# Linear attention and a feed-forward layer on one core: sums of g moved behind the fourth division, k^T v moved ahead of one product, a third way of computing block 2, and four sums of weights given to GpSimd

## The chip, the core and the metric

The kernel runs on one core of a Trainium2 chip. The core has a matrix engine (TensorE, "PE" in the profile, its weight loads "PEld"), a vector engine (VectorE, "DVE"), a scalar engine (ScalarE, "ACT"), GpSimd ("POOL") and a queue engine (SyncE, "SP"), each of which works through its own instructions in their written order. They wait for each other by semaphores. [...] The metric is the device time of one execution in microseconds (us), taken as the median of several; lower is better.

## The reference

With B = 8 batches, H = 8 heads, S = 576 positions and D = 64, the attention is linear, with cosine and sine weights by position; behind it stand two matrix products with a gelu between them:

```
phi(x) = concat(relu(x) * cos_w, relu(x) * sin_w)          # 64 -> 128 features
kv = phi(k)^T v ;  z = sum over positions of phi(k)
x  = (phi(q) kv) / (phi(q) z + 1e-6)                       # (8, 576, 512) -> 4608 tokens of 512
h  = x @ w_in                                              # 512 -> 2048
g  = h * sigmoid(1.702 h)
out = g @ w_out                                            # 2048 -> 512, (4608, 512) float32
```

## The kernel before, in words

A block is a batch. Of its 576 tokens 512 are worked on in the block; the last 64 of each batch are collected in `xt` and are the tail, done after all blocks. The order of all instructions is written out by hand (`manual_schedule`): what stands earlier in the program comes earlier in its engine's queue.

The blocks are staggered. While block b is in its matrix products, the attention of block nb = b + 1 is prepared: `trig` (L169) makes the weighted relu of k on VectorE, `vcopy` (L193) converts v, `trig_q` (L183) makes that of q on ScalarE, and `qturn_dma` (L219) turns it with a transposing DMA from SP's queue. `kv_next` opens a PSUM tile of the pool `pat` (name `at`), makes k^T v in 72 small matmuls (L237) and has VectorE copy it to `kvs` (L245). Five times per block, `x_next(nb, c)` then does for 128 tokens: `num_mm` (eight matmuls, L310, into a tile of `pat`), `num_div` (VectorE: L321 adds eps to the denominators, L323 inverts, L325 multiplies and writes `xn`) and `xturn_dma` (L354), a transposing DMA that writes the x of the next block. The pool `pat` has two buffers, so `num_mm` number c waits until VectorE has done with the division of number c - 2.

The first product of a block, x @ w_in, is done in 16 column groups fc of 128 columns. In the plain way (`mm1_part` at L365, `mm1_at` at L721) a group is four matmuls of 128 x 512. Blocks 3 to 6 (the range `PAIR`) use *units* instead for groups 0 to 3 and 8 to 11 (`mm1_pair`, class `Unit`): a form of fast matrix multiplication in which two units U and V make seven products (`step(1)` to `step(7)`, four matmuls of 128 x 256 each, L658) where the plain way needs eight. It needs sums of blocks of w_in (`win_sum`, L621 to L627, made once and kept in `ws_pair`, which lies in the buffer `gt`) and of blocks of x (`x_pair`, `x_sum`, L635 to L641, made for each block at the end of the block before). Between the products, ScalarE copies partial results (`snap`, L672) and VectorE adds (`add`, L667); the gelu of a unit reads such a sum (L663). Groups 4 to 7 and 12 to 15 remain plain. Block 2 does all 16 groups in the plain way, and during it VectorE makes the four sums of w_in.

The second product, g @ w_out, is done with seven products too (`wino_mm`, L520), in the order of `PRODUCTS`: p1, p2, p6, p5, p7, p3, p4. Each has two halves c, so the program counts s = 0 to 13. p6, p5, p7 and p3 take as their weights the sums s2, s1, s3 and s4 of blocks of g, which VectorE makes in `g_sums` (L473, L475, L477, L479), each in two halves h of 128 x 1024. `wino_after` has ScalarE keep a partial result (`keep`, L535) or VectorE join two into an output (`join`, L545); the output leaves by a DMA from GpSimd's queue (L526).

In a block of PAIR the last steps are, as written: `V.step(5)`, the plain group 14, `V.step(3)`, `kv_next`, the plain group 15, each with its gelu, then s1 and s2 for h = 0 and h = 1, `x_next(nb, 0)`, and the fourteen `wino_mm` with x_next 1 to 4 behind s = 1, 3, 4 and 6. The two halves of s3 stand behind s = 1, those of s4 behind s = 5.

Of the kernel before, what the change touches and what calls it, by code (L numbers as in the profile page):

```python
# [20 lines left out]
def kernel(  # L21
# [9 lines left out]
    nc = tc.nc  # L31
    B, H, S, D = q.shape
# [24 lines left out]
    def src_of(src, b, i0=0, i1=NI):  # L57
        return src[b, 2 * i0:2 * i1].rearrange("(i hh) (p j) d -> (hh p) i (j d)", hh=2, j=NS)

    qf = one.tile([128, 2560], F32, name="qf")  # L60
    kf, vf = [one.tile([128, NI, S], F32, name=n) for n in ("kf", "vf")]
# [62 lines left out]
    def load(t, src, b, eng=nc.gpsimd):  # L124
        eng.dma_start(out=t, in_=src_of(src, b))
# [7 lines left out]
    def load_q(b, eng=nc.gpsimd):  # L133
        load_chunks(qf, q, b, eng)
# [5 lines left out]
    def wcol(kc, fc):  # L140

        g, c = divmod(fc, 4)
        w = w_in_t[g][:, kc, :] if g < 2 else w_in_t[2][:, kc, ts(g - 2, 512)]
        return w.rearrange("p (f c) -> p f c", c=4)[:, :, c]
# [216 lines left out]
    def mm1_part(b, fc, t0, t1):  # L361
        if t0 == 0:
            hp[fc] = pmm.tile([128, MT], F32, name="mm")
        for kc in range(KC):
            nc.tensor.matmul(hp[fc][:, t0:t1], wcol(kc, fc), x[b][:, kc, t0:t1],  # L365
                             start=(kc == 0), stop=(kc == KC - 1))
# [99 lines left out]
    def g_sums(names, h, of=MAIN):  # L466

        tt = nc.vector.tensor_tensor
        a_blk, to = of
        o = {n: to[n][:, ts(h, 4)] for n in to}  # L470
        for n in names:
            if n == "s1":
                tt(o[n], a_blk(1, h), a_blk(1, h + 2), op=ADD)  # L473
            elif n == "s2":
                tt(o[n], o["s1"], a_blk(0, h), op=SUB)  # L475
            elif n == "s3":
                tt(o[n], a_blk(0, h), a_blk(1, h), op=SUB)  # L477
            else:
                tt(o[n], a_blk(0, h + 2), o["s2"], op=SUB)  # L479
# [119 lines left out]
    ws = {}  # L599
# [12 lines left out]
        slot_no[0] += 1  # L612
        return slots[slot_no[0] % 8].rearrange("p (f t) -> p f t", f=2)

    def win_sum(n, i, ws=ws):
        tt = nc.vector.tensor_tensor
        o = {m: ws[m][:, :, ts(i, 512)] for m in ws}
        a = {(0, k): w_in_t[i][:, ts(k, 2), :] for k in range(2)}
        a.update({(1, k): w_in_t[2][:, ts(k, 2), ts(i, 512)] for k in range(2)})
        if n == "s1":  # L620
            tt(o[n], a[1, 0], a[1, 1], op=ADD)  # L621
        elif n == "s2":
            tt(o[n], o["s1"], a[0, 0], op=SUB)
        elif n == "s3":
            tt(o[n], a[0, 0], a[1, 0], op=SUB)
        else:
            tt(o[n], a[0, 1], o["s2"], op=SUB)  # L627
# [15 lines left out]
    class Unit:  # L643
# [31 lines left out]
        def step(self, p):  # L675
# [17 lines left out]
            else:  # L693
# [2 lines left out]

    PAIR = range(3, B - 1)
    gt_flat = gt.rearrange("p f e -> p (f e)")  # L700
    ws_pair = {n: gt_flat[:, ts(i, 1024)].rearrange("p (k f) -> p k f", k=2)
               for i, n in enumerate(("s1", "s2", "s3", "s4"))}
# [15 lines left out]
    def mm1_at(b, fc):  # L718
        hp[fc] = pat.tile([128, 2, 512], F32, name="at")[:, 0]
        for kc in range(KC):  # L720
            nc.tensor.matmul(hp[fc], wcol(kc, fc), x[b][:, kc], start=(kc == 0), stop=(kc == KC - 1))  # L721
        gelu(fc, True)

    def mm1_pair(b, nb):
        for qd in (0, 2, 1, 3):
            gT[qd] = gpool.tile([128, 4, MT], BF16, name="g")
        banks4 = [pmm.tile([128, 512], F32, name="mm") for _ in range(4)]
        U, V = [Unit(b, u, banks4[u], banks4[2], banks4[3], ws_pair, xp[b], pair_slot) for u in range(2)]
        ks = iter(range(NS))

        def k_next(n):
            for _ in range(n):
                trig(kr, kf, next(ks))

        U.step(1)
        V.step(1)
        k_next(3)
        mm1_at(b, 4)
        mm1_at(b, 5)
        U.step(2)  # L740
        k_next(4)
        U.step(6)
        V.step(6)
        U.gelu(0, 0, U.c11)
        mm1_at(b, 6)
        mm1_at(b, 7)
        V.step(2)
        k_next(2)
        if nb + 1 < B:
            load_q(nb + 1, nc.sync)  # L750
            load(kf, k, nb + 1, nc.sync)
        U.step(7)
        U.step(5)
        V.gelu(0, 0, V.c11)
        V.step(7)
        mm1_at(b, 12)
        U.gelu(1, 1, U.c22)
        U.step(4)
        U.gelu(1, 0, U.A)
        vcopy(0, 2)  # L760
        U.step(3)
        vcopy(2, 4)
        V.step(4)
        V.gelu(1, 0, V.A)
        U.gelu(0, 1, U.c12)
        mm1_at(b, 13)
        V.step(5)
        mm1_part(b, 14, 0, MT)
        V.gelu(1, 1, V.c22)
        V.step(3)  # L770
        gelu(14)
        kv_next()
        mm1_part(b, 15, 0, MT)
        V.gelu(0, 1, V.c12)
        gelu(15)
        g_sums(("s1", "s2"), 0)
# [16 lines left out]
    def kv_next():  # L793
        kv_mm_next()
        kv_evac(0, 4)
# [169 lines left out]
    def x_next(b, c):  # L965
        num_mm(c)
        num_div(c)
        xturn_dma(b, c)


    for b in range(1, B):
        nb = b + 1 if b + 1 < B else None
        if nb is None:
            break
        f0 = 5 if b == 1 else 0
        if b in PAIR:
            mm1_pair(b, nb)
        for fc in range(f0, FC) if b not in PAIR else ():
            if b == 1 and fc == f0:
                for c in range(5):  # L980
                    trig_q(c)
                    qturn_dma(c)
            if nb is not None and fc == f0 + 1:
                kv_operands(nb)

                if nb + 1 < B:
                    if b == 1:
                        load(kf, k, nb + 1, nc.sync)
                    load_q(nb + 1, nc.sync)
                    if b > 1:  # L990
                        load(kf, k, nb + 1, nc.sync)
                if b == 2:
                    for n in ws_pair:
                        win_sum(n, 0, ws_pair)
            if fc == 8 and b == 1:
                vcopy()
            if fc == 12:
                if b > 1:
                    g_sums(("s3",), 0)
                    g_sums(("s3",), 1)  # L1000
                g_sums(("s1", "s2", "s4") if b > 1 else ("s1", "s2"), 0)
            if fc == 14 and nb is not None and b > 1:
                kv_next()
            mm1(b, fc)
        if nb is not None:
            x_open(nb)
            if b == 2:
                x_next(nb, 0)
            if b == 1:
                kv_mm_next()  # L1010
            g_sums(("s1", "s2"), 1)
            if b > 2:
                x_next(nb, 0)
            if b == 1:
                kv_evac(0, 4)
                g_sums(("s3",), 0)
            at = ({2: [0], 3: [1], 4: [2], 6: [3], 8: [4]} if b == 1 else
                  {2 * p + 1: [p + 1] for p in range(4)} if b == 2 else
                  {s: [p + 1 if nb < B - 1 else (4, 1, 2, 3)[p]] for p, s in enumerate((1, 3, 4, 6))})
            wino_open()  # L1020
            for p in range(7):
                for c in range(2):
                    wino_mm(p, c)
                    s = 2 * p + c
                    if c == 1:
                        wino_after(b, p)
                    for c2 in at.get(s, ()):
                        x_next(nb, c2)
                        if c2 == 3 and nb + 1 < B:
                            load(vf, v, nb + 1, nc.sync)  # L1030

                    s0 = 4 if b > 2 else 8
                    if s0 <= s < s0 + 5 and nb + 1 < B:
                        trig_q(s - s0, act=True)
                    if 8 <= s < 13 and nb + 1 < B:
                        qturn_dma(s - 8)
                    if s == 1 and b == 2:
                        g_sums(("s4",), 1)
                    if s == 1 and b > 2:
                        g_sums(("s3",), 0)  # L1040
                        g_sums(("s3",), 1)
                    if s == 5 and b > 2:
                        g_sums(("s4",), 0)
                        g_sums(("s4",), 1)
                    if s == 2 and b == 1:
                        g_sums(("s3",), 1)
                    if s == 4 and b == 1:
                        g_sums(("s4",), 0)
                    if s == 6 and b == 1:
                        g_sums(("s4",), 1)  # L1050
            if nb in PAIR:
                x_pair(nb)
# [3 lines left out]
    b = B - 1  # L1056
# [103 lines left out]
```

## Time and profile before

| what | value |
|---|---|
| median of 3 runs | 277.41 us (277.34 to 277.67) |
| the profiled execution | 277.53 us, span of its instructions 275.6 us |
| PE busy | 267.9 us (97% of the span), clock granted in full in all slices |
| VectorE busy | 203.0 us (74%) |
| ScalarE busy | 172.8 us (63%) |
| GpSimd busy | 43.0 us (16%), most of it issuing DMAs |
| block 1, second product | from 67.07 to 80.56 us on PE |
| block 2 | from 80.56 to 109.12 us on PE |
| block 3 | from 109.12 to 137.61 us on PE |
| tail and block 7 | from 223.24 us on |

Times in the views of the trace count from the start of the span. A row of the timeline merges equal neighbouring instructions of one engine: start, length, engine, line, operation, names of what is written and read, sizes, and how many; in brackets the idle time before it and what ended it. The ends of matmuls are modelled and overlap the next start, so on PE the distances between starts are to be read. The chain is the sequence of work, followed back from the last instruction, that ended last.

### The profile page before, as it was taken

How to read it: one execution, taken by the hardware profiler on the slowest of the kernel's cores; microseconds unless marked ns; L12 is line 12 of the kernel's file. 1: busy time of each engine (PE TensorE's matmuls, PEld its weight loads, DVE VectorE, ACT ScalarE, POOL GpSimd, SP SyncE). 2: the span in 40 equal slices, each digit the busy share in tenths (PEclk: the TensorE clock that was granted, in tenths of full speed). 3: DMA queues.
4: the chain of work that ended last, by engine and by line, in shares of the span. 5: the costliest groups of instructions: out<-in, count | busy, mean ns of one | idle time of the engine just before them, and what ended most of it. 6: DMA issues, size and time to landing. Idle time of an engine off the chain costs nothing.

```text
span 275.6 us, 6999 instructions
## 1 busy us (share of the span) xinstructions
PE 267.9 (97%) x2844; PEld 204.5 (74%) x2844; DVE 203.0 (74%) x476; ACT 172.8 (63%) x311; POOL 43.0 (16%) x71
## 2 busy tenths in 40 slices
PE   8899999999999999999999999999999999999994
PEld 2585645856975699778877887788778876999983
DVE  4943775698899596879887988888888985744741
ACT  6967642584297519974788387848683147677621
POOL 5691000000122012100210022001200163000310
PEclk9999999999999999999999999999999999999999
DMA  7999999999999897997799689999991754000233
GB/s 232 253 211 298 278 295 162 255 305 197 301 207 289 225 262 192 255 242 206 187 299 233 195 114 278 170 284 194 236 196 23 107 149 139 0 0 2 82 111 114
DMA packets 73663, 53.60 MB, mean 194 GB/s; under 512 B 52736, under 2 KB 63488, under 8 KB 73632
## 3 DMA queue, kind: packets, MB, share of 16 engines
q1 hardware_dynamic: 67504, 36.97, 60.9%
q0 software_dynamic: 6128, 16.19, 22.6%
q8 instruction: 22, 0.36, 0.6%
q14 instruction: 9, 0.07, 0.1%
HBM read 36.70 MB, written 9.44 MB: 167 GB/s over the span
## 4 chain that ended last, share of the span: by engine, by line
PE 81%; DVE 12%; DMA 4%; issue 1%; ACT 0%; POOL 0%
PE mm L520 22%; PE mm L365 16%; PE mm L658 14%; PE at L721 8%; PE mm L421 5%; PE at L520 4%; PE mm L396 4%; PE at L237 4%; DVE xn L325 3%; DMA sums<-in_v_dram 2%; DVE sums L475 2%; PE at L310 2%; DVE sums L477 2%; DVE sums L473 2%; DMA kf<-in_k_dram 1%; DVE inv L323 1%
## 5 line engine op out<-in xcount | busy, mean ns | idle before, releaser
L365 PE MATMUL mm<-xT,w_in 128*128 128x512 bf16 (+1 forms) x304 | 51.4, 320 | 0.0
L526 POOL DMA_DIRECT2D out_dram<-ysb x24 | 18.1, 754 | 182.0 <-DVE den L321 124.6
L520 PEld LDWEIGHTS <-sums 128*128 128x128 bf16 x448 | 42.5, 98 | 4.6
L371 ACT ACTIVATE g<-mm 128x512 bf16<-128x512 f32 x56 | 32.2, 597 | 14.6 <-PE mm L365 14.6
L365 PEld LDWEIGHTS <-w_in 128*128 128x128 bf16 x304 | 27.6, 114 | 17.3
L520 PE MATMUL mm<-wsum,sums 128*128 128x256 bf16 x336 | 39.9, 272 | 0.0
L520 PEld LDWEIGHTS <-g 128*128 128x128 bf16 x336 | 32.0, 98 | 3.6
L169 DVE TENSOR_SCALAR kr<-kf,cosw 128x256 bf16<-128x256 f32 x69 | 24.5, 355 | 5.3 <-DMA kf<-in_k_dram 5.3
L325 DVE TENSOR_TENSOR xn<-at,inv 128x512 bf16<-128x512 f32 x39 | 27.0, 691 | 1.3
L520 PE MATMUL mm<-w_out_sb,g 128*128 128x256 bf16 x224 | 26.6, 273 | 0.0
L169 DVE TENSOR_SCALAR kr<-kf,sinw 128x256 bf16<-128x256 f32 x68 | 23.5, 345 | 0.0
L721 PE MATMUL at<-xT,w_in 128*128 128x512 bf16 x96 | 23.3, 379 | 0.0
L183 ACT ACTIVATE qn<-qf,cosw 128x512 bf16<-128x512 f32 (+1 forms) x27 | 19.2, 712 | 2.2 <-DMA qf<-in_q_dram 2.2
L183 ACT ACTIVATE qn<-qf,sinw 128x512 bf16<-128x512 f32 (+1 forms) x27 | 19.2, 710 | 0.0
L535 ACT ACTIVATE kept_p<-mm 128x512 f32<-128x512 f32 (+1 forms) x15 | 8.5, 566 | 16.7 <-PE mm L520 14.9
L658 PE MATMUL mm<-xT,w_in 128*128 128x256 bf16 x128 | 18.6, 273 | 0.0
L658 PEld LDWEIGHTS <-w_in 128*128 128x128 bf16 x144 | 15.9, 113 | 2.7
L310 PEld LDWEIGHTS <-qT 128*128 128x128 bf16 x312 | 13.8, 97 | 5.1 <-issue 3.7
L658 PE MATMUL mm<-xT,gt 128*128 128x256 bf16 x128 | 17.2, 272 | 0.0
L310 PE MATMUL at<-kvs,qT 128*128 128x65 bf16 x312 | 15.7, 193 | 1.3 <-DVE den L321 1.3
L535 ACT ACTIVATE kept_u<-mm 128x512 f32<-128x512 f32 (+1 forms) x8 | 4.4, 544 | 18.8 <-PE mm L520 15.4
L658 PEld LDWEIGHTS <-gt 128*128 128x128 bf16 x128 | 14.1, 113 | 2.4 <-issue 0.9
(175 smaller groups left out, 452.6 us busy)
## 6 DMA issues: line engine op xcount, KB each, us to landing
kf<-in_k_dram SPq DMA_DIRECT2D x6, 1152.0 KB, 9.1
vf<-in_v_dram SPq DMA_DIRECT2D x6, 1152.0 KB, 7.0
qf<-in_q_dram SPq DMA_DIRECT2D x6, 1024.0 KB, 6.5
out_dram<-ysb POOLq DMA_DIRECT2D x24, 256.0 KB, 5.5
w_out_sb<-in_moe_w_out_dram POOLq DMA_DIRECT2D x4, 512.0 KB, 17.2
kf<-in_k_dram POOLq DMA_DIRECT2D x1, 1152.0 KB, 13.1
vf<-in_v_dram POOLq DMA_DIRECT2D x1, 1152.0 KB, 20.3
w_in<-in_moe_w_in_dram POOLq DMA_DIRECT2D x2, 512.0 KB, 10.0
```

Source lines behind the costliest of these rows:

```text
L169: eng.tensor_scalar(o, i, 0.0, w[:, j:j + 1], op0=MAX, op1=MUL)
L183: nc.scalar.activation(o, i, AF.Relu, scale=sc)
L310: nc.tensor.matmul(ps[:, h // 4, ds((h % 4) * 65, 65)], qT[:, h, ts(c, 128)], kvs_of(h), start=not eps_too, stop=(not eps_too or h % 4 == ...
L325: nc.vector.tensor_tensor(xn, pv[:, :, :, 0:64], inv.unsqueeze(3).to_broadcast([128, 2, 4, 64]), op=MUL)
L365: nc.tensor.matmul(hp[fc][:, t0:t1], wcol(kc, fc), x[b][:, kc, t0:t1], start=(kc == 0), stop=(kc == KC - 1))
L371: nc.scalar.activation(gT[fc // 4][:, fc % 4], hp.pop(fc), AF.Gelu_apprx_sigmoid)
L421: nc.tensor.matmul(yp[b, t, c0][:, c0:c1], w, w_out_sb[:, fc, c0:c1], start=(fc == 0), stop=(fc == FC - 1))
L520: nc.tensor.matmul(bank[to][c], lhs, rhs, start=opens, stop=(fc == HF - 1), skip_group_check=True)
L526: eng.dma_start(out=dst[:, 2 * i + c0:2 * i + c1, ts(n, HD)], in_=t[:, c0:c1])
L535: nc.scalar.activation(o, i, AF.Identity)
L658: nc.tensor.matmul(to[:, j], lhs, rhs, start=(opens and j == 0 and k == 0), stop=(k == 1), skip_group_check=True)
L721: nc.tensor.matmul(hp[fc], wcol(kc, fc), x[b][:, kc], start=(kc == 0), stop=(kc == KC - 1))
```

## The change

Four edits:

1. In blocks with units, both halves of s3 and of s4 are made behind s = 4, which is behind the fourth division (`x_next` number 3), in place of behind s = 1 and s = 5.
2. In `mm1_pair`, `kv_next` stands ahead of `V.step(3)` and not behind it.
3. `PAIR` begins at block 2, so that block 2 is done with units too. What was written for block 2 alone goes: its own places for `kv_next`, for the sums of g and for `x_next`. The sums of x for block 2 are made at the end of block 1.
4. The four sums of w_in that all blocks with units share are made by GpSimd: s1 and s2 behind s = 0 of block 1's second product, s3 behind s = 4, s4 behind s = 8.

```diff
-    def win_sum(n, i, ws=ws):
-        tt = nc.vector.tensor_tensor
+    def win_sum(n, i, ws=ws, eng=nc.vector):
+        tt = eng.tensor_tensor
...
-    PAIR = range(3, B - 1)
+    PAIR = range(2, B - 1)
...
         V.gelu(1, 1, V.c22)
-        V.step(3)
         gelu(14)
         kv_next()
+        V.step(3)
         mm1_part(b, 15, 0, MT)
         V.gelu(0, 1, V.c12)
         gelu(15)
...
                 if nb + 1 < B:
-                    if b == 1:
-                        load(kf, k, nb + 1, nc.sync)
+                    load(kf, k, nb + 1, nc.sync)
                     load_q(nb + 1, nc.sync)
-                    if b > 1:
-                        load(kf, k, nb + 1, nc.sync)
-                if b == 2:
-                    for n in ws_pair:
-                        win_sum(n, 0, ws_pair)
...
             if fc == 12:
-                if b > 1:
-                    g_sums(("s3",), 0)
-                    g_sums(("s3",), 1)
-                g_sums(("s1", "s2", "s4") if b > 1 else ("s1", "s2"), 0)
-            if fc == 14 and nb is not None and b > 1:
-                kv_next()
+                g_sums(("s1", "s2"), 0)
             mm1(b, fc)
         if nb is not None:
             x_open(nb)
-            if b == 2:
-                x_next(nb, 0)
             if b == 1:
                 kv_mm_next()
             g_sums(("s1", "s2"), 1)
-            if b > 2:
+            if b > 1:
                 x_next(nb, 0)
...
             at = ({2: [0], 3: [1], 4: [2], 6: [3], 8: [4]} if b == 1 else
-                  {2 * p + 1: [p + 1] for p in range(4)} if b == 2 else
                   {s: [p + 1 if nb < B - 1 else (4, 1, 2, 3)[p]] for p, s in enumerate((1, 3, 4, 6))})
...
-                    if s == 1 and b == 2:
-                        g_sums(("s4",), 1)
-                    if s == 1 and b > 2:
-                        g_sums(("s3",), 0)
-                        g_sums(("s3",), 1)
-                    if s == 5 and b > 2:
-                        g_sums(("s4",), 0)
-                        g_sums(("s4",), 1)
+                    if s == 4 and b > 1:
+                        for n in ("s3", "s4"):
+                            g_sums((n,), 0)
+                            g_sums((n,), 1)
+                    if b == 1:
+                        for n in {0: ("s1", "s2"), 4: ("s3",), 8: ("s4",)}.get(s, ()):
+                            win_sum(n, 0, ws_pair, nc.gpsimd)
```

In GpSimd's queue the sums s1 and s2 of w_in stand behind the loads of the weights and ahead of the first output DMA of block 1; s3 and s4 stand between that DMA and the second one.

## The prediction, made before the changed kernel ran

> **What bounds the kernel now.** I read the page first:
>
> ```profile
> PE 267.9 (97%) x2844; PEld 204.5 (74%) x2844; DVE 203.0 (74%) x476; ACT 172.8 (63%) x311; POOL 43.0 (16%) x71
> ```
>
> TensorE is the bound at a clock granted in full, so the time can change in two ways: fewer or cheaper matmuls, or more or less waiting between them. Then I read the timeline of TensorE, by distances between starts, over the blocks. Block 2 (plain) runs from 80.56 to 109.12, 28.56 us; block 3 (units) from 109.12 to 137.61, 28.49 us; the chain shows the starts of blocks 4, 5, 6 and of the tail at 137.78, 166.27, 194.75 and 223.24 (by its own ends), so all blocks with units are alike.
>
> ```profile
> 80.56 12.25 PE L365 MATMUL mm<-xT,w_in 128*128 128x512 bf16 x56
> ...
> 109.12 1.04 PE L658 MATMUL mm<-xT,w_in 128*128 128x256 bf16 x8
> ```
>
> ```profile
> 121.02 0.60 PE L658 MATMUL mm<-xT,gt 128*128 128x256 bf16 x4
> 121.55 1.26 PE L237 MATMUL at<-vt,kr 64*128 64x65 bf16 x72
> 122.75 1.05 PE L365 MATMUL mm<-xT,w_in 128*128 128x512 bf16 x4
> 123.70 0.40 PE L310 MATMUL at<-kvs,qT 128*128 128x65 bf16 x8
> ...
> 127.67 0.41 PE L310 MATMUL at<-kvs,qT 128*128 128x65 bf16 x8
> ...
> 131.26 0.40 PE L310 MATMUL at<-kvs,qT 128*128 128x65 bf16 x8 [0.32 <-DVE den L321]
> 131.50 2.78 PE L520 MATMUL mm<-wsum,sums 128*128 128x256 bf16 x24
> ...
> 137.61 1.04 PE L658 MATMUL mm<-xT,w_in 128*128 128x256 bf16 x8
> ```
>
> This is the seam in block 3, between the units and the second product. Sixteen matmuls of 128x256 take 1.75 us from start to start, four of 128x512 take 0.87. By that, TensorE loses 0.48 us ahead of 131.26, where `num_mm(4)` waits for the third division, 0.13 ahead of V.step(3) at 121.02 (it waits for VectorE's sum of step 5), and 0.06 ahead of 123.70. Third, VectorE and ScalarE there:
>
> ```profile
> 121.66 0.69 DVE L667 TENSOR_TENSOR kept_u<-kept_u,mm 128x512 f32<-128x512 f32 x1 [0.69 <-PE mm L658]
> 122.85 0.70 DVE L245 CAST kvs<-at 128x520 bf16<-128x520 f32 x1 [0.51 <-PE at L237]
> 123.47 0.68 DVE L473 TENSOR_TENSOR sums<-g 128x1024 bf16<-128x1024 bf16 x1
> ...
> 126.55 0.69 DVE L325 TENSOR_TENSOR xn<-at,inv 128x512 bf16<-128x512 f32 x1
> ...
> 128.20 1.28 DVE L477 TENSOR_TENSOR sums<-g 128x1024 bf16<-128x1024 bf16 x2
> ...
> 130.42 0.69 DVE L325 TENSOR_TENSOR xn<-at,inv 128x512 bf16<-128x512 f32 x1
> ```
>
> ```profile
> 122.38 0.63 ACT L663 ACTIVATE g<-kept_u 128x512 bf16<-128x512 f32 x1 [0.26 <-DVE kept_u L667]
> ```
>
> From 122.85 VectorE never rests: kvs, four sums of g, two divisions, s3 twice, a join, two divisions. Here VectorE, not TensorE, sets the pace. And the first sum needs the gelu of V.step(3) (the ACT row), which is early: over at 123.01, while s1 starts at 123.47.
>
> **The change, part by part.** Seam of a block with units, by block 3's rows.
>
> *TensorE.* Group 14 starts at 120.02 as before and takes 0.87. k^T v may start 0.09 later (such a gap stands ahead of 121.55 too), at 120.98, and takes 1.20, to 122.18. V.step(3), now behind it, takes 0.44, to 122.62; the 0.13 us wait goes, since VectorE's sum is over at 120.97. Group 15 ends at 123.49 and `num_mm(0)` starts there, 0.21 earlier than 123.70; kvs is ready at 122.98.
>
> *The price.* What V.step(3) feeds is late: VectorE's sum (0.64 behind the step's start; the kvs copy, 122.28 to 122.90, is queued ahead of it) starts at 122.90, not 121.66. The gelu starts 0.72 later, 123.62, and ends at 124.25, with gelu 15 queued behind it. The first sum of g, and behind it all of VectorE's queue, starts at 124.30, not 123.47: 0.83 later. The first division's last step starts 3.08 behind that, 127.38, and ends at 128.07; `num_mm(2)` may start 0.15 later (as 131.26 stands to 130.42 + 0.69), at 128.22. TensorE is there at 123.49 + (127.67 - 123.70) = 127.46. New stall: 0.76 us.
>
> *What edit 1 gives.* Without s3 in between, the third division ends at 124.30 + 6.45 = 130.75, and TensorE reaches `num_mm(4)` at 131.33: the old 0.48 is gone. But the four late sums start only at 131.70; the halves of s3 end at 132.38 and 132.98, and p7 wants them at 132.44 and 0.44 later: with 0.15 of latency each, 0.25 us lost. s4 (134.18) is in time. p7's last twelve matmuls (1.31), p3 and p4 (1.75 each) follow from 133.13 and end at 137.94. Before it was 137.61: **+0.32 us per block**, 1.3 for blocks 3 to 6. Bounds: the gelu's sum directly behind step 3 (122.82) makes it +0.22; 0.15 more between ScalarE and VectorE makes it +0.47.
>
> *Block 2.* Thirty-two matmuls of 128x512 at 0.216 (6.9 us) become 56 of 128x256 at 0.109 (6.1): -0.79 of TensorE's work. But block 2 had no wait at its seam (its `num_mm` rows follow without a gap), and gets the new ones: 28.49 + 0.32 = 28.81 for 28.56, **+0.25** (+0.15 to +0.4). Its four sums of x (1.47 on VectorE, rows 136.67 to 138.14) start when the last xT has landed (80.52) and are needed 3.04 into the block: hidden. ScalarE's q work of block 1 ends at 82.29, so the first snap starts at 82.77 and is over 0.2 before step 6 needs it: hidden; without that 0.2 it costs what is late. VectorE sheds four sums of w_in (86.26 to 88.79), off the path: nothing. SP's loads of q and k come from another place but stand behind the same five transposes of qT (to 91.35): nothing.
>
> *GpSimd's sums.* s1 and s2 run from about 24.8, long before use; VectorE then works on k alone. s3 and s4 start behind the output DMA of 72.76, at 73.5, while VectorE makes block 1's own s4 of g:
>
> ```profile
> 72.76 0.71 POOL L526 DMA_DIRECT2D out_dram<-ysb x1 [48.01 <-DVE den L321]
> ```
>
> ```profile
> 76.09 0.68 DVE L479 TENSOR_TENSOR sums<-g,sums 128x1024 bf16<-128x1024 bf16 x1
> ```
>
> ```profile
> 77.02 1.91 PE L520 MATMUL mm<-w_out_sb,sums 128*128 128x256 bf16 x16
> ```
>
> Nearest rows to the length of one: GpSimd's copy of 128x1024 bf16, 1.05 us (the row below), and its TENSOR_SCALAR of 128x256, 1.14, four times which is 4.6. Two inputs read in turn at the copy's pace make 2.1; I take 2.2, nearest to the copy in size and type. And the trace shows what such an operation does to a sum on VectorE:
>
> ```profile
> 222.14 1.28 DVE L621 TENSOR_TENSOR kf<-w_in 128x1024 bf16<-128x1024 bf16 x2
> ...
> 224.54 2.56 DVE L625 TENSOR_TENSOR vf<-w_in,w_in 128x1024 bf16<-128x1024 bf16 x2
> ```
>
> ```profile
> 224.90 1.05 POOL L1057 COPY gt<-gt 128x1024 bf16<-128x1024 bf16 x1
> ```
>
> The same two sums took 1.28 us longer beside a copy of 1.05, while the divisions at 15.87 and 17.59 (one input in PSUM) kept their 0.69 beside GpSimd's work. So VectorE's s4, h = 0, issued at 74.45, waits until 75.7; h = 1, issued near 77.3, waits for GpSimd's s4 (to 77.9 or 78.5) and ends at 78.6 to 79.2. p3 needs it at 77.46: 1.3 to 1.9 lost. The fourth join, which p4 waits for, ends at 80.2 to 80.85 where p4 was due at 78.77: 1.5 to 2.2 in all. I take **+1.9**. Bounds: a sum of 1.05 us is out of the way in time, 0; one of 4.7 keeps s4 until 84.2, +6.9; if GpSimd starts its second sum before VectorE gets in, 3.2.
>
> [...]
>
> Sum: 4 x 0.32 + 0.25 + 1.9 = +3.4 us. The profiled execution (277.53) lies 0.12 above the median; on the median: **280.8 us**.
>
> **The rivals.**
>
> *A, the forecast*: 280.8; by its bounds 279.6 to 282.6.
>
> *B, GpSimd disturbs nothing*: its sums are short, or fall between VectorE's. For it: s3 needs only 1 us less to be clear of h = 0. Against it: the 2.56 row. Then +1.5: 278.9.
>
> *C, faster: the first sum of g does not wait for the late gelu.* Place: 123.47 in block 3. If the path from V.step(3) to s1 is as short as the copy of kvs, s1 starts near 123.5 and each block ends 13.63 later (137.94 - 124.30), at 137.16: -0.45 in four blocks, -0.52 in block 2, 275.1. It decides from a start of s1 at 123.98 on. Against it: sum, gelu and their starts add up to 2.1 us behind step 3's start, each by a row. With GpSimd's 1.9 on top it would be 277.0, no difference.
>
> *D, GpSimd's sums take 4.7 us each*: 277.4 + 1.5 + 6.9 = 285.8. For it: its TENSOR_SCALAR; against it: its copy.
>
> **How the numbers follow.** A 0.55, B 0.21, C alone 0.11, C with GpSimd's cost 0.07, D 0.06. A change within 0.2% (0.55 us) can't be told from none. Faster 0.11; the same 0.07; slower 0.82. The predicted time is A's, 280.8. The range takes in A, B and C with GpSimd's cost and leaves out C alone and D, 0.17: 277.0 to 282.6; A's own is 279.6 to 282.6.
>
> **What would show it.** In the changed profile: in each block with units, k^T v without a wait ahead of V.step(3); s1 0.8 us later against group 14 than now; a wait of some 0.75 us ahead of the third `num_mm` of a block and a small one inside p7, none ahead of the fifth; blocks 3 to 6 of 28.8 us, block 2 of the same length; L479 rows of block 1 far over 0.68 us beside GpSimd's L625 and L627, and p3 of block 1 waiting for them. I am wrong if s1 starts as early as now, if GpSimd's sums leave the L479 rows at 0.68, or if they take twice as long as I say.

## The result, and the profile after

The changed kernel takes 281.45 us (median of 6 runs, 281.43 to 282.7); the kernel before takes 277.47 beside it (6 runs). The ratio is 1.0151, with a 95% interval of 1.0133 to 1.0168: it is slower, by 0.65 us more than the 280.8 that was forecast, and inside the range. The profiled execution has a span of 279.4 us, 3.7 longer than before.

Two lines of the page of the changed kernel, its busy times and the chain that ended last by engine:

```profile
PE 267.1 (96%) x2847; PEld 206.1 (74%) x2868; DVE 210.2 (75%) x483; ACT 175.0 (63%) x317; POOL 50.8 (18%) x75
...
PE 72%; DVE 18%; DMA 4%; issue 2%; ACT 2%; SPq 1%
```

TensorE has about as much to do as before. Its weight loads rise by 24 (2844 to 2868), as 32 wide matmuls of block 2 become 56 narrow ones; of the matmuls only 2847 are recorded, 21 too few, so the 0.8 us of difference in its busy time can't be read as block 2's saving. VectorE's share of the chain is 18%; on the page of before it was 12%. More of the end is now set by VectorE. Where, the timeline of TensorE tells. First the end of block 1:

```profile
76.00 1.04 PE L520 MATMUL mm<-wsum,sums 128*128 128x256 bf16 x8
78.20 0.61 PE L520 MATMUL mm<-w_out_sb,sums 128*128 128x256 bf16 x4 [1.17 <-DVE sums L479]
79.84 1.48 PE L520 MATMUL mm<-w_out_sb,sums 128*128 128x256 bf16 x12 [1.03 <-DVE sums L479]
81.47 1.91 PE L520 MATMUL mm<-wsum,g 128*128 128x256 bf16 x16
83.22 1.04 PE L658 MATMUL mm<-xT,w_in 128*128 128x256 bf16 x8
```

By starts, at 0.109 us a matmul of 128x256, eight end at 76.87 and p3 begins at 78.20, 1.33 late; its first four end at 78.64 and the other twelve begin at 79.84, another 1.20 late; they end at 81.15 and p4 begins at 81.47, 0.32 late. That is 2.85 us. VectorE and GpSimd in the same stretch, first VectorE's rows, then GpSimd's:

```profile
74.31 3.84 DVE L479 TENSOR_TENSOR sums<-g,sums 128x1024 bf16<-128x1024 bf16 x1
...
79.10 0.68 DVE L479 TENSOR_TENSOR sums<-g,sums 128x1024 bf16<-128x1024 bf16 x1
```

```profile
73.38 2.14 POOL L625 TENSOR_TENSOR gt<-w_in,w_in 128x1024 bf16<-128x1024 bf16 x1
75.46 2.13 POOL L627 TENSOR_TENSOR gt<-w_in,gt 128x1024 bf16<-128x1024 bf16 x1
```

The reader is to see that VectorE's sum, 0.68 us when it is alone, is open from 74.31 until 78.15, while GpSimd works without a pause until 77.59. It stood through both of GpSimd's sums, not through one. The division of the next tokens, the second half of s4 and the fourth join are queued behind it.

Now the seam of block 3. TensorE, then VectorE, then the gelu of V.step(3) on ScalarE:

```profile
122.84 1.03 PE L365 MATMUL mm<-xT,w_in 128*128 128x512 bf16 x4
123.80 1.26 PE L237 MATMUL at<-vt,kr 64*128 64x65 bf16 x72
124.99 0.63 PE L658 MATMUL mm<-xT,gt 128*128 128x256 bf16 x4
...
126.32 0.41 PE L310 MATMUL at<-kvs,qT 128*128 128x65 bf16 x8
...
128.55 1.91 PE L520 MATMUL mm<-w_out_sb,g 128*128 128x256 bf16 x16
131.02 0.40 PE L310 MATMUL at<-kvs,qT 128*128 128x65 bf16 x8 [0.56 <-DVE den L321]
...
134.12 0.41 PE L310 MATMUL at<-kvs,qT 128*128 128x65 bf16 x8
134.36 2.96 PE L520 MATMUL mm<-wsum,sums 128*128 128x256 bf16 x24
137.15 1.91 PE L520 MATMUL mm<-w_out_sb,sums 128*128 128x256 bf16 x16
...
140.65 0.60 PE L658 MATMUL mm<-xT,w_in 128*128 128x256 bf16 x4
```

```profile
125.10 0.70 DVE L245 CAST kvs<-at 128x520 bf16<-128x520 f32 x1 [1.32 <-PE at L237]
125.71 0.68 DVE L667 TENSOR_TENSOR gt<-gt,mm 128x512 f32<-128x512 f32 x1
127.09 0.69 DVE L473 TENSOR_TENSOR sums<-g 128x1024 bf16<-128x1024 bf16 x1 [0.70 <-ACT g L663]
...
130.18 0.69 DVE L325 TENSOR_TENSOR xn<-at,inv 128x512 bf16<-128x512 f32 x1
...
134.50 1.28 DVE L477 TENSOR_TENSOR sums<-g 128x1024 bf16<-128x1024 bf16 x2
```

```profile
126.42 0.63 ACT L663 ACTIVATE g<-gt 128x512 bf16<-128x512 f32 x1 [1.49 <-DVE gt L667]
```

k^T v now starts without a wait ahead of V.step(3). But the sum of step 3 is queued behind the kvs copy, its gelu ends at 127.05, and the first sum of g starts at 127.09, with VectorE idle for 0.70 us ahead of it. Group 14 starts at 122.84 here, so s1 starts 4.25 behind it; before it was 3.45 (123.47 - 120.02). That is 0.80 later, and the third `num_mm` pays for it: by starts TensorE loses 0.73 ahead of 131.02. Ahead of 134.12, where before lost 0.48, nothing is lost. The row at 134.36 holds eight matmuls of p5 and the sixteen of p7, which need 2.62; the next row starts at 137.15. Some 0.15 is lost there, ahead of the last twelve matmuls of p7, which use the second half of s3.

Stretches on TensorE from start to start, in us:

| | before | after | difference |
|---|---|---|---|
| block 1, second product | 13.49 | 16.31 | +2.82 |
| block 2 | 28.56 | 28.72 | +0.16 |
| blocks 3 to 6, each | 28.49 | 28.72 | +0.23 |

That is 2.82 + 0.16 + 4 x 0.23 = 3.90; block 1's second product starts 0.16 earlier, which leaves 3.74, the difference of the spans. The medians differ by 3.98.

### The profile page after: what moved, and what is told of

The parts are those of the page before. It is cut to its first block, busy times and chain, and to the rows that moved or that the text cites. A ratio compares the mean times of both kernels' runs of the same rounds, so it can differ in the third digit from the quotient of the medians.

```text
span 279.4 us, 7045 instructions
## 1 busy us (share of the span) xinstructions
PE 267.1 (96%) x2847; PEld 206.1 (74%) x2868; DVE 210.2 (75%) x483; ACT 175.0 (63%) x317; POOL 50.8 (18%) x75
## 4 chain that ended last, share of the span: by engine, by line
PE 72%; DVE 18%; DMA 4%; issue 2%; ACT 2%; SPq 1%
PE mm L520 22%; PE mm L658 15%; PE at L721 9%; PE mm L365 6%; PE at L520 4%; PE mm L396 4%; PE mm L421 4%; PE at L237 4%; DVE sums L475 3%; DVE sums L473 3%; DVE kr L169 2%; DVE xn L325 2%; DMA qf<-in_q_dram 2%; DMA kf<-in_k_dram 2%; PE at L310 2%
## 5 line engine op out<-in xcount | busy, mean ns | idle before, releaser
L520 PEld LDWEIGHTS <-sums 128*128 128x128 bf16 x448 | 41.5, 98 | 9.1 <-DVE sums L479 2.8
L365 PE MATMUL mm<-xT,w_in 128*128 128x512 bf16 (+1 forms) x239 | 38.6, 304 | 0.5
L365 PEld LDWEIGHTS <-w_in 128*128 128x128 bf16 x248 | 21.7, 113 | 11.2
L721 PE MATMUL at<-xT,w_in 128*128 128x512 bf16 x110 | 27.8, 380 | 0.5
L371 ACT ACTIVATE g<-mm 128x512 bf16<-128x512 f32 x42 | 24.0, 595 | 6.8 <-PE mm L365 6.8
L169 DVE TENSOR_SCALAR kr<-kf,sinw 128x256 bf16<-128x256 f32 x68 | 25.4, 373 | 0.0
L658 PE MATMUL mm<-xT,w_in 128*128 128x256 bf16 x152 | 22.0, 273 | 0.0
L658 PE MATMUL mm<-xT,gt 128*128 128x256 bf16 x160 | 21.7, 273 | 0.0
L658 PEld LDWEIGHTS <-w_in 128*128 128x128 bf16 x168 | 18.5, 113 | 3.4
L721 PEld LDWEIGHTS <-w_in 128*128 128x128 bf16 x120 | 13.5, 113 | 8.2
L371 ACT ACTIVATE g<-at 128x512 bf16<-128x512 f32 x30 | 17.8, 598 | 2.5 <-PE at L721 1.7
L658 PEld LDWEIGHTS <-gt 128*128 128x128 bf16 x160 | 17.2, 114 | 1.5
```

The costliest lines, as they stand in the source:

```text
L169: eng.tensor_scalar(o, i, 0.0, w[:, j:j + 1], op0=MAX, op1=MUL)
L371: nc.scalar.activation(gT[fc // 4][:, fc % 4], hp.pop(fc), AF.Gelu_apprx_sigmoid)
L520: nc.tensor.matmul(bank[to][c], lhs, rhs, start=opens, stop=(fc == HF - 1), skip_group_check=True)
L658: nc.tensor.matmul(to[:, j], lhs, rhs, start=(opens and j == 0 and k == 0), stop=(k == 1), skip_group_check=True)
```

## The experiments

The theory after the result has two parts. First, GpSimd's s3 and s4 of w_in cost what they cost because they stand beside VectorE's own sums at the end of block 1. Second, k^T v ahead of V.step(3) costs each block with units, while late sums of g are a gain by themselves. Rivals: GpSimd's sums are innocent and block 1 is longer for other reasons (the sums of x at its end, another order of transfers); or the late sums of g are what costs; or it is only that GpSimd writes to SBUF (the memory on the core that holds the tiles), or that it reads there at all.

All results in one table. The ratio is to the kernel before, on the same chip, with its 95% interval; e9 and e10 ran on another chip than e1 to e8, so across these the ratios are to be compared. The stretches are those of the table above, each from one profiled execution.

| run | what it is | us | ratio | block 1 | block 2 | blocks 3 to 6 |
|---|---|---|---|---|---|---|
| after | all four edits | 281.45 | 1.0151 (1.0133 to 1.0168) | 16.31 | 28.72 | 28.72 |
| e1 | after, GpSimd's sums all early | 278.60 | 1.0032 (1.0021 to 1.0042) | 13.45 | 28.72 | 28.72 |
| e2 | after, edit 2 undone | 277.97 | 1.0025 (1.0010 to 1.0040) | 16.31 | 28.01 | 28.02 to 28.11 |
| e3 | e1 and e2 together | 275.33 | 0.9919 (0.9903 to 0.9935) | 13.45 | 28.01 | 28.01 to 28.11 |
| e4 | before, edit 1 alone | 275.60 | 0.9923 (0.9907 to 0.9939) | 13.45 | 28.56 | 28.01 to 28.11 |
| e5 | before, edit 2 alone | 280.67 | 1.0113 (1.0092 to 1.0134) | 13.87 | 28.56 | 29.31 |
| e6 | before, edit 4 alone | 280.61 | 1.0118 (1.0088 to 1.0148) | 16.31 | 28.57 | 28.49, one 28.85 |
| e7 | e1, GpSimd only writes there | 278.86 | 1.0051 (1.0033 to 1.0069) | 13.44 | 28.95 | 28.72 |
| e8 | e1, GpSimd copies there | 278.98 | 1.0060 (1.0040 to 1.0080) | 13.93 | 28.72 | 28.72 |
| e9 | e1, division ahead of the sums of g | 275.78 | 0.9947 (0.9933 to 0.9961) | 13.45 | 28.14 | 28.14 to 28.23 |
| e10 | after, one of GpSimd's sums later | 279.99 | 1.0088 (1.0071 to 1.0105) | 14.22 | 29.40 | 28.71 |

### e1: all of GpSimd's sums early

```diff
-                        for n in {0: ("s1", "s2"), 4: ("s3",), 8: ("s4",)}.get(s, ()):
+                        for n in {0: ("s1", "s2", "s3", "s4")}.get(s, ()):
```

> The changed kernel, with all four sums of w_in on GpSimd behind s = 0 of block 1, so that s3 and s4 run right behind s1 and s2 near 29 to 33.5 us and not beside VectorE's s4 of g at 74 us. Theory (the contention in block 1 is a matter of place): block 1's second product is back from 16.3 to 13.5 us, the total falls by 2.8 us from 281.45 to 278.6 us; one two-input sum of VectorE (L442 near 31.5 us) gets longer, hidden. Rival (a sum on GpSimd costs the same wherever it stands): no change, 281.4 us.

Measured: 278.60 us, 2.85 less than after. The first timeline is VectorE's and the second TensorE's, at the end of block 1:

```profile
74.04 0.68 DVE L479 TENSOR_TENSOR sums<-g,sums 128x1024 bf16<-128x1024 bf16 x1
```

```profile
80.10 1.04 PE L658 MATMUL mm<-xT,w_in 128*128 128x256 bf16 x8
```

The same program with the same number of instructions, only with two of them elsewhere in GpSimd's queue, has VectorE's sum back at 0.68 and block 1 back at 13.45. Block 1's loss is GpSimd's two sums at that place and nothing else. e1 also showed a loss that nobody pays for: where the four sums now stand, VectorE makes the weighted relu of k (first its rows, then GpSimd's):

```profile
26.91 2.21 DVE L169 TENSOR_SCALAR kr<-kf,sinw 128x256 bf16<-128x256 f32 x1
29.05 2.22 DVE L169 TENSOR_SCALAR kr<-kf,cosw 128x256 bf16<-128x256 f32 x1
31.19 2.23 DVE L169 TENSOR_SCALAR kr<-kf,sinw 128x256 bf16<-128x256 f32 x1
33.34 0.34 DVE L169 TENSOR_SCALAR kr<-kf,cosw 128x256 bf16<-128x256 f32 x1
```

```profile
28.94 2.18 POOL L625 TENSOR_TENSOR gt<-w_in,w_in 128x1024 bf16<-128x1024 bf16 x1
31.08 2.19 POOL L627 TENSOR_TENSOR gt<-w_in,gt 128x1024 bf16<-128x1024 bf16 x1
```

Each of the first three operations, 0.34 us alone, lasts as long as one of GpSimd's sums. They lose 1.9 us each, and TensorE starts block 2 at 80.10 all the same: k has that much time in block 1. The expectation had named another victim, the two-input sum L442; that one is pushed back to 37.01, behind GpSimd's sums, and keeps its 1.22.

### e2 and e3: k^T v back behind V.step(3), without and with e1

```diff
         V.gelu(1, 1, V.c22)
+        V.step(3)
         gelu(14)
         kv_next()
-        V.step(3)
         mm1_part(b, 15, 0, MT)
```

> The changed kernel with k^T v back behind V.step(3) (edit 2 undone, the others kept). Theory (the seam got slower only because V.step(3), and with it the gelu that s1 of g waits for, is late): s1 is 0.8 us earlier, the 0.73 us wait ahead of the third num_mm and the 0.15 us in p7 go, the old wait of 0.48 us ahead of the fifth num_mm doesn't come back; blocks 2 to 6 take 28.0 us, the total falls by 5 x 0.7 to 277.9 us. Rival (the late s3 and s4 of edit 1 cost the seam as well): blocks stay at or above 28.5 us, 280 us or more.

> The changed kernel with both: all GpSimd sums behind s = 0, and k^T v behind V.step(3). Theory: the two costs lie in different stretches and add, 281.45 - 2.8 - 3.5 = 275.1 us, faster than both kernels. Rival (the gain of one is eaten by a wait that the other hides): 277 us or more.

Measured: 277.97 and 275.33 us. Against after, undoing edit 2 gives 3.48, e1 gives 2.85, and both give 6.12: the two costs are apart from each other and nearly add up. e3 is faster than the kernel before, and its median is the lowest of the study (that of e4, 275.60, can't be told from it). TensorE in the seam of its block 3, and below it the chain of its page:

```profile
120.71 1.26 PE L237 MATMUL at<-vt,kr 64*128 64x65 bf16 x72
...
126.83 0.41 PE L310 MATMUL at<-kvs,qT 128*128 128x65 bf16 x8
...
129.94 0.41 PE L310 MATMUL at<-kvs,qT 128*128 128x65 bf16 x8
...
136.33 1.04 PE L658 MATMUL mm<-xT,w_in 128*128 128x256 bf16 x8
```

```profile
PE 92%; DMA 5%; POOL 1%; DVE 0%; ACT 0%; issue 0%
```

No `num_mm` behind the first waits any more. What is left of the seam is, by starts, 0.12 ahead of V.step(3), which edit 2 was able to remove, and 0.09 ahead of the first `num_mm`. VectorE has left the chain.

### e4 and e5: edit 1 alone, edit 2 alone

e4, from the kernel before:

```diff
-                    if s == 1 and b > 2:
-                        g_sums(("s3",), 0)
-                        g_sums(("s3",), 1)
-                    if s == 5 and b > 2:
-                        g_sums(("s4",), 0)
-                        g_sums(("s4",), 1)
+                    if s == 4 and b > 2:
+                        for n in ("s3", "s4"):
+                            g_sums((n,), 0)
+                            g_sums((n,), 1)
```

> The kernel before with edit 1 alone: s3 and s4 of g behind the fourth division in blocks 3 to 6. Theory: VectorE's third division is 1.2 us earlier, the wait of 0.48 us ahead of the fifth num_mm goes and nothing replaces it: 4 x 0.48 = 1.9 us less, 275.5 us. Rival (late sums make p7 wait by themselves): no gain, 277.4 us or more.

e5, from the kernel before, is the exchange of `V.step(3)` and `kv_next()` alone.

> The kernel before with edit 2 alone: k^T v ahead of V.step(3) in blocks 3 to 6. Theory: s1 of g is 0.8 us late, so is all of VectorE's queue behind it, and with s3 still ahead of the third division each of the four blocks ends 0.8 us later: +3.2 us, 280.7 us, with waits ahead of the third and of the fifth num_mm. Rival (the earlier kvs and the saved wait ahead of V.step(3) pay for it): 276.7 to 277.5 us.

Measured: 275.60 and 280.67 us. The late sums of g are a gain of 0.44 us in each of the four blocks. k^T v ahead of V.step(3), alone, costs 0.82 in each. TensorE in block 3 of e5:

```profile
128.23 0.40 PE L310 MATMUL at<-kvs,qT 128*128 128x65 bf16 x8 [0.56 <-DVE den L321]
...
132.10 0.40 PE L310 MATMUL at<-kvs,qT 128*128 128x65 bf16 x8 [0.61 <-DVE den L321]
```

By starts the third `num_mm` loses 0.73 and the fifth another 0.77 (0.48 in the kernel before): with s3 in its old place VectorE has no slack in which to catch up. In the changed kernel edit 1 removes the second of these waits; it does not reach the first, which stands ahead of the place where s3 was. So the two edits are not neutral to each other: the first gains 0.44 alone, the second costs 0.82 alone and 0.67 beside the first (28.05 in e3, 28.72 in e1).

e5 has 0.42 more in block 1 as well, which no edit of it touches: its block 2 starts at 80.58, after 0.25 us of idle time for a transposed x. That is one execution.

### e6: edit 4 alone

From the kernel before: the four `win_sum` of block 2 go, and GpSimd makes them in block 1 as in the change (`win_sum` takes the engine as there). Block 2 remains plain.

```diff
-                if b == 2:
-                    for n in ws_pair:
-                        win_sum(n, 0, ws_pair)
...
+                    if b == 1:
+                        for n in {0: ("s1", "s2"), 4: ("s3",), 8: ("s4",)}.get(s, ()):
+                            win_sum(n, 0, ws_pair, nc.gpsimd)
```

> The kernel before with edit 4 alone: the four sums of w_in by GpSimd at the places of the changed kernel, block 2 still plain. Theory: VectorE's first s4 of g in block 1 takes some 3.8 us, p3 and p4 of block 1 wait, +2.8 us, 280.3 us; the 2.5 us of VectorE's time saved in block 2 are worth nothing. Rival (the loss in block 1 comes from the sums of x for block 2 or another part of edit 3): no change, 277.5 us.

Measured: 280.61 us. VectorE's first half of s4 in block 1:

```profile
74.10 3.84 DVE L479 TENSOR_TENSOR sums<-g,sums 128x1024 bf16<-128x1024 bf16 x1
```

It is the same 3.84 us, and the same 16.31 for the stretch. Without units in block 2 there are no sums of x for it at the end of block 1, so these have no part in the loss. Block 2 takes 28.57 without its four sums of w_in on VectorE and 28.56 with them: they were off the path there, and giving them away gained nothing.

### e7 and e8: GpSimd writes only, GpSimd reads one input

e1, and in the place of GpSimd's s3 and s4, behind s = 4 and s = 8, two operations each on a part of `gt` that nothing reads at that time. e7 writes zeros, e8 copies from w_in:

```diff
+                        if s in (4, 8):
+                            for r in range(2):
+                                nc.gpsimd.memset(gt_flat[:, ds(4096 + (s // 4) * 1024, 1024)], 0.0)
```

> The changed kernel with all four sums behind s = 0, and at s = 4 and s = 8 in their place two GpSimd memsets of 128x1024 bf16 each into a part of gt that nothing uses then (about as long, and they write SBUF but read nothing). Theory (GpSimd's reading of SBUF is what a two-input sum on VectorE excludes): VectorE's L479 stays at 0.68 us, 278.6 us. Rival (any GpSimd work, or its holding of SBUF's write side, blocks VectorE): L479 takes 2 to 4 us, 280 to 281.5 us.

> As the run with memsets, with two GpSimd copies of 128x1024 bf16 in place of the two memsets (they read one SBUF input, about 1.05 us each). Theory: reading is enough, VectorE's first L479 of block 1 waits until the copies are over, 281 us; if VectorE gets in between two of them, 279 to 280 us. Rival (only a GpSimd operation with two inputs excludes it): L479 at 0.68 us, 278.6 us.

Measured: 278.86 and 278.98 us, for e1's 278.60. VectorE in e7, then GpSimd in e7, then VectorE and GpSimd in e8:

```profile
74.10 0.68 DVE L479 TENSOR_TENSOR sums<-g,sums 128x1024 bf16<-128x1024 bf16 x1
```

```profile
73.15 3.88 POOL L1032 MEMSET gt<- 128x1024 bf16 x4
```

```profile
74.14 0.68 DVE L479 TENSOR_TENSOR sums<-g,sums 128x1024 bf16<-128x1024 bf16 x1
...
75.78 1.47 DVE L479 TENSOR_TENSOR sums<-g,sums 128x1024 bf16<-128x1024 bf16 x1
```

```profile
73.20 4.95 POOL L1032 COPY gt<-w_in 128x1024 bf16<-128x1024 bf16 x4
```

Writing for 3.9 us without a pause holds neither of VectorE's two sums (the second, at 75.74, takes 0.68 as well): that rival falls. Reading does, but four copies cost less than the 279 to 280 us expected for the case that VectorE gets in between them: VectorE's first sum is not held, the second loses 0.79, and the stretch grows by 0.48 (13.45 to 13.93). The four copies last 4.95 together, 0.75 more than four times the 1.05 that a copy of this size took in the kernel before. VectorE's sums are over at 74.82 and 77.25, the last copy at 78.15: between copies VectorE gets its turn. Between the two sums of after it did not. (Block 2 of e7 is 0.23 longer than in e1. Its sums of x wait for a transposed x until 80.48, in e1 until 79.86; that this is the whole reason is not shown. The one block of 28.85 in e6 stays open.)

### e9: the first division ahead of the sums of g

From e1, so k^T v stays ahead. VectorE's queue begins the seam with `x_next(nb, 0)`, then s1 and s2; s3 stands behind s = 3 and s4 behind s = 4. If what hurts is that the divisions wait for a late gelu, this takes the divisions out of its way.

```diff
-        g_sums(("s1", "s2"), 0)
...
-            g_sums(("s1", "s2"), 1)
+            if b == 1:
+                g_sums(("s1", "s2"), 1)
             if b > 1:
                 x_next(nb, 0)
+                g_sums(("s1", "s2"), 0)
+                g_sums(("s1", "s2"), 1)
...
-                    if s == 4 and b > 1:
-                        for n in ("s3", "s4"):
+                    if s in (3, 4) and b > 1:
+                        for n in ("s3",) if s == 3 else ("s4",):
```

> The changed kernel with all GpSimd sums behind s = 0, k^T v still ahead of V.step(3), but in VectorE's queue the first division of a block ahead of s1 and s2 of g, s3 behind the third division and s4 behind the fourth. Theory (the price of edit 2 is VectorE's queue standing behind a sum that waits for the late gelu, not k^T v's place itself): the first division fills that wait, the 0.73 us ahead of the third num_mm go, some 0.3 us ahead of the fourth num_mm take their place; blocks 2 to 6 take 28.1 us, the total is 275.3 to 275.9 us. Rival (moving k^T v ahead costs TensorE or ScalarE directly): blocks stay at 28.7 us, 278.6 us.

Measured: 275.78 us. VectorE in block 3, then TensorE:

```profile
123.72 0.69 DVE L325 TENSOR_TENSOR xn<-at,inv 128x512 bf16<-128x512 f32 x1
124.33 0.68 DVE L473 TENSOR_TENSOR sums<-g 128x1024 bf16<-128x1024 bf16 x1
```

```profile
128.24 0.40 PE L310 MATMUL at<-kvs,qT 128*128 128x65 bf16 x8 [0.15 <-DVE xn L325]
```

The late gelu costs nothing when a division stands between it and s1: VectorE goes from one to the other without a pause, and the third `num_mm` is in time. One wait of 0.31 by starts stands ahead of the fourth. e9 also makes s3 one step sooner (L477 at 129.64), but that is behind the third `num_mm`, which starts at 126.81 without a wait, so it can't be what removed the 0.73. So the price of edit 2 is the order in VectorE's queue, not k^T v's place on TensorE. With the order mended, edit 2 is no gain but nearly no loss: 28.14 to 28.23 a block, for 28.01 to 28.11 without it in e3.

### e10: GpSimd's two sums apart

From after, the s4 of w_in behind s = 10 and not s = 8, so that a DMA issue that waits for a join stands between the two.

```diff
-                        for n in {0: ("s1", "s2"), 4: ("s3",), 8: ("s4",)}.get(s, ()):
+                        for n in {0: ("s1", "s2"), 4: ("s3",), 10: ("s4",)}.get(s, ()):
```

> The changed kernel with GpSimd's s4 of w_in behind s = 10, so that only one of its sums (s3, 2.14 us) stands in VectorE's s4 of g, and the other falls behind the output DMA of p7, near 79.5 us. Theory (VectorE's sum waits for as long as GpSimd's sums follow each other): the first L479 of block 1 takes 1.8 to 1.9 us in place of 3.84, p3 waits 0.4 us at most, 278.6 to 279.2 us. Rival (the wait has a cause that one sum is enough for): L479 near 3.8 us, 281 us or more.

Measured: 279.99 us, more than expected. VectorE, then GpSimd:

```profile
74.86 1.77 DVE L479 TENSOR_TENSOR sums<-g,sums 128x1024 bf16<-128x1024 bf16 x1
...
81.33 2.04 DVE L635 TENSOR_TENSOR xT<-xT 128x512 bf16<-128x512 bf16 x1 [0.81 <-DMA xT<-xn]
```

```profile
73.94 2.13 POOL L625 TENSOR_TENSOR gt<-w_in,w_in 128x1024 bf16<-128x1024 bf16 x1
...
80.95 2.14 POOL L627 TENSOR_TENSOR gt<-w_in,gt 128x1024 bf16<-128x1024 bf16 x1
```

The part that it was made for came as expected: beside one sum of GpSimd, VectorE's sum takes 1.77 us, not 3.84; that the other 2.07 is the second sum (2.13 long) is shown. The time was missed because the moved sum only found another victim: at 80.95 it stands beside the first sum of x for block 2, which takes 2.04 in place of 0.42. VectorE's work of block 2 is late by that, and TensorE loses 0.73 ahead of the row below: block 2 takes 29.40 for 28.72. And 1.77 in place of 0.68 still cost block 1 0.73 (0.45 in p3, 0.31 ahead of p4).

```profile
91.11 0.60 PE L658 MATMUL mm<-xT,gt 128*128 128x256 bf16 x4 [0.56 <-DVE gt L667]
```

## Why the prediction was nearly right

**GpSimd's sums in block 1: said +1.9, measured +2.82.** This is the mis-sized term. The mechanism (VectorE's s4 of g held by GpSimd's s3 and s4 of w_in) is shown by e1, e6 and e10, and the length of one sum was well estimated, 2.2 us for 2.14. What failed is the step "VectorE's s4, h = 0 ... waits until 75.7": I let VectorE in between GpSimd's two sums, then had the second half wait for the second sum. It was not let in; h = 0 stood through both, until 78.15, and h = 1 then took its plain 0.68. The prediction had this as a bound, at 3.2; measured 2.82. In e10, with the two sums apart, the first half took 1.77, near the 1.9 that the step had assumed (74.45 to 75.7, and 0.64 for the sum itself).

Beside the memsets of e7, which read nothing, VectorE's sum took 0.68 us; beside GpSimd's sums, which read two inputs each, it took 3.84 (after) and 1.77 (e10). In both it ended 0.56 behind the last of the sums that it stood beside: at 78.15 for 77.59, and at 76.63 for 76.07. On who is next when one engine waits and the other has a second instruction ready, the runs go both ways: VectorE got in between copies (e8, 0.68 and 1.47) and not between two sums (after, 3.84).

**The seam of blocks 3 to 6: said +0.32 each, measured +0.23.** Step by step, behind the start of group 14: the first `num_mm` at 3.47 said and 3.48 measured; s1 0.83 later said, 0.80 measured; the wait ahead of the third `num_mm` 0.76 said, 0.73 measured; the wait ahead of the fifth gone, as said. p7 was to lose 0.25 and lost 0.15. The prediction took 0.15 from the end of a VectorE sum to the matmuls that use it, a figure that it had read behind a division. Block 1's rows give 0.05 and 0.06 for a sum (78.15 to 78.20, 79.78 to 79.84). With 0.06 the prediction's own times have the first half of s3 ready when p7 wants it (132.44) and the second 0.16 late (133.04 for 132.88). That accounts for the difference. Two readings are off in the second digit and change nothing: the wait ahead of 123.70 is 0.08 by its rows, not 0.06, and 137.94 less 137.61 is 0.33.

**Block 2: said +0.25, measured +0.16.** It has the length of the other blocks (28.72), as forecast; the 0.09 is the same p7 again. The sums of x, the first snap and the loads hid as said.

**What was costed at nothing.** VectorE's four sums of w_in out of block 2: nothing, by e6. GpSimd's s1 and s2 beside "VectorE then works on k alone": the cover was thought to be undisturbed and isn't. In the changed kernel one operation on k, at 27.01, takes 2.25 us for 0.34 beside the second of these sums (26.99 to 29.11); with all four sums there, e1's rows show 1.9 us lost three times, 5.7 in all. The price is nothing all the same: block 1's second product starts no later.

**The rivals.** B (GpSimd disturbs nothing) falls by 3.84 for 0.68, D (4.7 us a sum) by 2.14. C said that s1 would not be late, and that a block would then be 0.45 shorter. s1 was 0.80 late, so C falls; but e3, where V.step(3) is back in its place, has blocks of 28.01 to 28.11, 0.38 to 0.48 shorter than before. Its size was right and its condition was what edit 2 took away. The two errors of the sum, +0.9 in block 1 and -0.45 in five seams, partly cancelled.

What stays open is why VectorE gets its turn between GpSimd's copies (e8) and between GpSimd's sums when it holds a one-input operation (e1, 26.91 to 33.4), and not between L625 and L627 with a two-input sum. No run changed only the kind of VectorE's operation.

Edit 3 was not run without edit 4. From e4 to e3 block 2 goes from 28.56 to 28.01, which is what units there are worth in the profiled executions once the seam has no waits; in the medians it is not shown: 275.60 and 275.33 lie inside each other's spread.

## What to carry to other kernels

In these runs a sum handed to GpSimd was not simply taken off VectorE: while it read SBUF, it held a VectorE operation on SBUF for up to its whole length (3.84 us for 0.68 beside two sums, 2.21 for 0.34 beside one). Such work belongs beside work of VectorE that is due much later (e1), not beside a sum that TensorE is waiting for. When an instruction is moved ahead on the bounding engine to fill a gap of 0.13 us, look at who waits for what now comes behind it: here a gelu 0.8 us later held a whole in-order queue of VectorE, and cost five times the gap. Edits that come in one change should be priced one by one; this one held a gain of 2.1 us (e3) under two costs of 2.85 and 3.48.

## What the runs showed of the hardware that was not expected

A VectorE operation with one f32 input in SBUF and a bf16 output there, TENSOR_SCALAR of 128x256, was held by a two-input GpSimd sum as well: 2.21 us for 0.34 (e1, three times in a row). The rows of before had shown only that the divisions, which read PSUM (the memory of the tiles `mm` and `at`), were not held: 0.69 us at 15.87 and at 17.59, beside GpSimd's TENSOR_SCALAR of 15.46 to 17.79.

GpSimd lost time as well: its four copies of 1.05 us took 4.95 in place of 4.20 while two of VectorE's sums ran among them (e8). Four memsets of 128x1024 by GpSimd, 3.88 us in a row, left both sums of VectorE beside them at 0.68 (e7).
